# Batch 0 of a state-attention and Mish kernel: a finer hand-written order, word scaling for two slots at a time, and a state product in 256-column pieces

## The chip, the cores and the metric

The kernel runs on one core of a Trainium2 chip. The metric is the device time of one execution in microseconds (us). The median of three runs before the change is 707.46 us (705.67 to 708.41).

Five engines work side by side, each through its own queue in order: TensorE (PE: matrix products and transposes), VectorE (DVE), ScalarE (ACT: activations, copies, casts), GpSimd (POOL) and SyncE (SP), which here only issues DMAs. An engine waits at an instruction until what it needs is there, and all that stands behind it in its queue waits too.

## The reference

Two parts. First an attention between `x` (8 batches, 8 heads, 512 tokens, 64 wide) and a small `state` (32 rows per head), in both directions. Then a two-layer network over the joined result (8 x 544 rows, 512 wide, hidden 2048).

```python
scores  = scale * x @ state.T                 # per batch and head
a       = softmax(scores over the 32 state rows)
xread   = a @ state                           # 512 rows per head
scores2 = scale * state @ x.T
a2      = softmax(scores2 over the 512 tokens)
sread   = a2 @ x                              # 32 rows per head
rows    = concat([xread, sread], axis=2)      # -> (8 * 544, 512)

h   = rows @ w_in
out = (h * tanh(softplus(h))) @ w_out         # Mish, then the second product
```

Inputs are 64-bit floats; the result is 32-bit.

## The kernel before

**Weights.** `w_in` and `w_out` come as pairs of 32-bit words of 64-bit floats. The kernel makes 32-bit floats of them itself, in eight pieces each: `scale_high` (Prelu on the high word) and `round_low` (Copy with scale and bias on the low word) prepare the halves, and `join_words` on VectorE shifts and ors them together (`join_w_in`, `join_w_out`). For `w_out` a cast (`high_w_out`) and a subtraction (`low_w_out`) follow: products that need 32-bit accuracy are made of a high and a low part in the faster fp32r format, three matmuls for one.

**The state is folded into the weights.** The xread rows are never formed. `sw_slice(b, j)` multiplies batch `b`'s state, laid out as blocks by `state_blocks`, with piece `j` of `w_in` (the state product, tiles `swp`) and splits the result into `swh` (ACT) and `swl` (DVE). Eight small matmul positions of the array, 64 rows by 32 columns each, work side by side in it; one such fp32 matmul shows as two instructions. `gemm1(b, j)` then multiplies the transposed attention weights (`ah`, `al`) with it: twelve matmuls of 512 columns into two PSUM tiles `ph`. Mish on ACT makes `g` of them, DVE splits `g` into `gh` (cast) and `gl` (subtraction), and `gemm2` adds its product with piece `j` of `w_out` into four accumulators `acc`: 24 matmuls, six for each tile of 128 tokens. One `j` is called a slot; a batch has eight (`SLOTS`). The sread rows of all batches are collected in `srT` and go through the network at the end (`gemm1_s`).

**The attention of a batch** (`attention`): transposes of x, scores, the softmax over state rows (`soft1_...`), the softmax over tokens (`soft2_...`), its transposes (`e2_transposed`), the read-out (`sread`) and its transpose (`sreadT`). For batches 0 and 1, x is transposed on PE; from batch 2 on it is loaded in another layout (`xq`) and transposed on DVE.

**Buffers** that matter here: two PSUM tiles `m` serve all small products (transposes of x, scores, state product, read-out); two `ph`; one `g`; two each of `gh`, `gl`, `swh`, `swl`; one joined `w_out` piece (`wt`); five `t` for the attention's temporaries; two `raw` for pieces of `w_in` as loaded. A load into a `raw` buffer can be issued only when the piece in it has been joined, and all DMAs stand in SP's queue in the order in which they are written. Pieces 2 and 3 of `w_in` lie where `w_out` 6 and 5 come later, and `w_out` 7 comes where batch 0's x lies.

**The order.** The program is planned by a scheduler that orders instructions by its own estimate of time. For batch 0 that is overridden: while `InOrder.on` is true, each instruction of PE, DVE and ACT is made to follow the one traced before it on the same engine, so these three queues run in the order in which lines 586 to 665 call them. In slots 1 to 7 that is the same pattern each time: the words of one piece of `w_in` (`words`, two halves) and one of `w_out`, from slot 3 on the low half of `w_out` on GpSimd; the joins; two tiles of the slot before's second product; mish and `gh`; the next state product; the other two tiles; `low_w_out` and `gl`; the next first product. Pieces of batch 0's second softmax and of batch 1's attention are put in at slots 3 to 7. What belongs to batch 1 and later and is traced after `InOrder.on = False` is free: the planner may put it into the three queues wherever it finds room, also between the ordered instructions.

Prelu and Exp belong to one table of ACT, Mish to another, and changing costs an `ACT_TABLE_LOAD`; Copy and casts stand in either. `FILL` matmuls without use keep PE busy at the start.

From batch 1 on a slot leaves the second product `LAG` slots behind, and a state product covers two slots: 512 columns, 16 matmul instructions.

Of the kernel before, what the change touches and what calls it, by code (L numbers as in the profile page):

```python
# [30 lines left out]
def as_f32(ap):  # L31
    return ap.bitcast(F32)

# [27 lines left out]
def state_attention_mish_kernel(ctx, tc, x, state, w_in, w_out, out):  # L61
# [70 lines left out]
    def scale_words(raw, pool_rounds=False):  # L132
        if pool_rounds:
            round_low(raw, True)
        scale_high(raw)
        if not pool_rounds:
            round_low(raw)

# [81 lines left out]
    def attention(b, sn, xq=None):  # L220
# [4 lines left out]
        def x_transposed(c):  # L225
# [17 lines left out]
        def scores():  # L243

            pss = [misc(f"sc_{b}_{u}") for u in range(2)]
            for c in range(NC):
                o = slice(c * NS, (c + 1) * NS)
                for kc in range(2):
                    kp = slice(kc * 2 * P, (kc + 1) * 2 * P)
                    for u in range(2):  # L250
                        last["PE"] = pe.matmul(
                            pss[u][o, kp], bds[b][half(u), kc, o], xTs[c][half(u), kp],
                            start=True, stop=True)

# [3 lines left out]
            for u in range(2):  # L258
# [4 lines left out]
                else:  # L263
                    act.mul(o, i, 0.125)

# [14 lines left out]
        def soft2_e(kc):  # L280
            e2 = temp(f"e2_{b}_{kc}")
            sm = pool.tile([P, 1], F32, tag="sm", name=f"sm_{b}_{kc}")
            act.activation(e2, sc[kc], AF.Exp, bias=nms[kc], accum_out=sm)
            dve.tensor_scalar_add(sm, sm, 1e-9)
# [3 lines left out]

        def soft2(kc):
            soft2_m(kc)  # L290
            soft2_e(kc)

        def e2_transposed(kc):
            e2 = e2s[kc]
            pt = misc(f"e2p_{b}_{kc}")
            for t in range(NT):
                pe.transpose(pt[:, t * P:(t + 1) * P], e2[:, t * P:(t + 1) * P], ident)
            e2T[kc] = temp(f"e2T_{b}_{kc}", (P, NT, P))
            act.copy(e2T[kc].rearrange("p t n -> p (t n)"), pt)

        e1s = {}
# [4 lines left out]
        e1, small = [], {}  # L306
# [11 lines left out]
        def soft1_e():  # L318
            e1.extend(temp(f"e1_{b}_{kc}") for kc in two)
            for n in ("mx", "s1", "r1"):  # L320
                small[n] = [pool.tile([P, 16], F32, tag=n, name=f"{n}_{b}_{kc}") for kc in two]
            src = e1
            if b == 0:
                src = [misc(f"scT_{b}_{kc}") for kc in two]
            for kc in two:
                if b == 0:
                    transposed(src[kc], sc[kc])
                else:
                    dve.transpose(e1[kc], sc[kc])
            for kc in two:  # L330
                mx = small["mx"][kc]
                dve.tensor_reduce(mx, groups(src[kc]), AX.X, ALU.max)
                dve.tensor_sub(groups(e1[kc]), groups(src[kc]), wide(mx))
                act.activation(e1[kc], e1[kc], AF.Exp)

        def soft1_n():
            sm, r1 = small["s1"], small["r1"]

            def total(kc):
                dve.tensor_reduce(sm[kc], groups(e1[kc]), AX.X, ALU.add)  # L340

            def guard(kc):
                dve.tensor_scalar_add(sm[kc], sm[kc], 1e-9)

            def turn(kc):
                dve.reciprocal(r1[kc], sm[kc])

            def norm(kc):
                dve.tensor_mul(groups(e1[kc]), groups(e1[kc]), wide(r1[kc]))

            for step, kc in ((total, 0), (guard, 0), (total, 1), (turn, 0), (guard, 1), (norm, 0), (turn, 1), (norm, 1)):
                step(kc)

        def soft1_a():
            for kc in two:
                if b == 0:
                    at = ps_acc.tile([P, 512], F32, tag="acc", name=f"at_{b}_{kc}")
                    transposed(at, e1[kc])
                else:
                    at = temp(f"at_{b}_{kc}")  # L360
                    dve.transpose(at, e1[kc])
                hi = pool.tile([P, S], F32R, tag=f"ah{kc}", name=f"ah_{b}_{kc}")
                lo = pool.tile([P, S], F32R, tag=f"al{kc}", name=f"al_{b}_{kc}")
                act.copy(hi, at)
                dve.tensor_sub(lo, at, as_f32(hi))
                aT[kc] = (hi, lo)

        def soft1():
            soft1_e()
            soft1_n()  # L370
            soft1_a()

        def sread(kc):
            pr = misc(f"srp_{b}_{kc}")
            for t in range(NT):
                for h4 in range(4):
# [6 lines left out]
                    )  # L383
            if kc == 0:
# [3 lines left out]
        def sreadT():  # L388
            pt = misc(f"srTp_{b}")[:, :P]
            pe.transpose(pt, srd[0].rearrange("p k d -> p (k d)"), ident)  # L390
            ptv = pt.rearrange("p (c n) -> p c n", c=NC)
            hi, lo = (t[..., b * NS:(b + 1) * NS] for t in srT)
            act.copy(hi, ptv)
            dve.tensor_sub(lo, ptv, as_f32(hi))

        xt, s_, s1, s2, e2t, sr = x_transposed, scores, soft1, soft2, e2_transposed, sread
        own = dict(xt=xt, s=s_, s1e=soft1_e, s1n=soft1_n, s1a=soft1_a, m2=soft2_m, e2=soft2_e,
                   e2t=e2t, sr=sr, srT=sreadT, fill=fill, aT=aT)
        ahead = [
            lambda: (state_blocks(b, sn), xt(0), xt(1)),  # L400
            lambda: (xt(2), xt(3)),
            lambda: s_(),
            lambda: (s1(), s2(0), s2(1)),
        ]
        read = [
            lambda: (e2t(0), e2t(1)),
            lambda: sr(0),
            lambda: sr(1),
            lambda: sreadT(),
# [329 lines left out]
```

## Time and profile before

| | |
|---|---|
| Runs | 707.46 us median of 3 (705.67 to 708.41) |
| Profiled execution | 703.54 us, of which 701.8 lie between its first and last instruction (the span) |
| Granted TensorE clock | 0.997 |
| Busy, share of the span | PE 97%, weight loads 74%, DVE 49%, ACT 38%, POOL 1% |
| Batch 0 | first product at 20.5 us; batch 1's first product at 108.1 us |
| Loads | 32 MB read; 399 GB/s between 10 and 30 us, 30 to 46 between 70 and 100 |

A row of the timeline gives the start and length in us, the engine, the source line (here the recording helper's, so tiles tell more), the operation, the tiles out <- in with their shape, and how many were merged (x4). What stands in brackets is the engine's idle time just before and what ended it. Matmuls overlap: twelve of 0.39 us follow each other at 0.23. Groups and windows sum such rows.

### The profile page before, as it was taken

To read this page: it belongs to the slowest core of one execution; us is meant where nothing else is said; L and a number is where in the kernel's file an instruction comes from. 1 tells how busy PE (TensorE), PEld (TensorE's weight loads), DVE (VectorE), ACT (ScalarE), POOL (GpSimd) and SP (SyncE) were. 2 spreads that over 40 slices of the span, in tenths; PEclk is the share of its full clock that TensorE was granted. 3 is DMA by queue.
4 is the path that set the end of the run, shared out by engine and by line. 5 is a ranking of instruction groups with operands and counts; after the bars stand their busy time and mean duration, and the time that the engine had idled before them with its cause. 6 is when DMAs were issued, how large, how long until landed. Compare 5 with 4: busy or idle time off the path is not lost.

```text
span 701.8 us, 10128 instructions
## 1 busy us (share of the span) xinstructions
PE 681.9 (97%) x4194; PEld 516.0 (74%) x4194; DVE 346.9 (49%) x520; ACT 264.6 (38%) x417; POOL 8.0 (1%) x11
## 2 busy tenths in 40 slices
PE   8999877999999999999999999999999999999997
PEld 7777554777677777777777777777777788977785
DVE  4886578365438423753357333842374334332221
ACT  4987735235235312551146122631245123212110
POOL 0020000000000000000000000000000000000000
PEclk9999999999999999999999999999999999999999
DMA  9964210340213010311022011301010001001001
GB/s 329 389 246 131 37 25 2 88 97 0 66 66 49 7 61 20 83 23 61 5 82 41 19 42 65 49 8 61 10 52 0 1 1 61 1 5 26 1 0 61
DMA packets 74926, 41.56 MB, mean 59 GB/s; under 512 B 56192, under 2 KB 64384, under 8 KB 74880
## 3 DMA queue, kind: packets, MB, share of 16 engines
q1 hardware_dynamic: 74592, 40.85, 19.9%
q8 instruction: 33, 0.54, 0.3%
q14 instruction: 13, 0.11, 0.1%
q10 hardware_dynamic: 288, 0.07, 0.0%
HBM read 31.98 MB, written 8.91 MB: 58 GB/s over the span
## 4 chain that ended last, share of the span: by engine, by line
PE 94%; ACT 2%; DVE 2%; issue 0%; DMA 0%; POOL 0%; ACTq 0%; POOLq 0%; DVEq 0%
PE acc L53 51%; PE ph L53 25%; PE swp L53 5%; PE ph_s L53 3%; PE acc_s L53 3%; PE sc L53 1%; PE srp L53 1%; PE e2p L53 1%; DVE e L53 1%; PE st L53 1%; ACT L53 1%; ACT wir L53 1%; PE xTp L53 1%; PE warm L53 0%; DVE s L53 0%
## 5 line engine op out<-in xcount | busy, mean ns | idle before, releaser
L53 PE MATMUL acc<-wo,gh 128*128 128x512 f32 x1024 | 326.9, 400 | 0.0
L53 PEld LDWEIGHTS acc<-wo,gh 128*128 128x128 f32 x1024 | 188.2, 188 | 69.0 <-issue 23.0
L53 PE MATMUL acc<-wo,gl 128*128 128x512 f32 x512 | 201.7, 396 | 0.0
L53 ACT ACTIVATE g<-ph 128x512 f32<-128x512 f32 x128 | 74.2, 597 | 224.8 <-DVE gl L53 147.0
L53 DVE CAST gh<-g 128x1024 fp32r<-128x1024 f32 x64 | 44.2, 691 | 161.3 <-PE acc L53 142.6
L53 PEld LDWEIGHTS acc<-wo,gl 128*128 128x128 f32 x512 | 96.2, 188 | 23.4 <-DVE gl L53 0.8
L53 PE MATMUL ph<-ah,swh 128*128 128x512 f32 x256 | 84.8, 404 | 7.0 <-ACT swh L53 3.5
L53 DVE TENSOR_TENSOR gl<-g,gh 128x1024 fp32r<-128x1024 f32 x64 | 78.3, 1223 | 4.9
L53 PE MATMUL ph<-al,swh 128*128 128x512 f32 x256 | 79.9, 393 | 0.0
L53 PE MATMUL ph<-ah,swl 128*128 128x512 f32 x256 | 79.4, 392 | 0.0
L53 DVE TENSOR_TENSOR swl<-swp,swh 128x512 fp32r<-128x512 f32 (+1 forms) x72 | 42.5, 624 | 49.7 <-ACT swh L53 49.1
L53 PEld LDWEIGHTS ph<-ah,swh 128*128 128x128 f32 x256 | 47.7, 189 | 21.8 <-ACT swh L53 4.4
L53 ACT ACT_TABLE_LOAD x39 | 50.0, 1283 | 26.8 <-PE e2p L53 14.1
L53 PEld LDWEIGHTS ph<-al,swh 128*128 128x128 f32 x256 | 48.3, 189 | 11.2 <-DVE xT L53 0.8
L53 PEld LDWEIGHTS ph<-ah,swl 128*128 128x128 f32 x256 | 47.7, 188 | 10.7
L53 ACT CAST swh<-swp 128x512 fp32r<-128x512 f32 (+1 forms) x72 | 35.6, 547 | 24.5 <-PE swp L53 24.5
L53 PE MATMUL swp<-w_in_sb,bd 64*32 64x512 f32 (+1 forms) x576 | 39.9, 554 | 0.4 <-DVE w_in_sb L53 0.3
L53 DVE TENSOR_TENSOR wl<-w_in_sb,wh 128x512 fp32r<-128x512 f32 x16 | 11.1, 692 | 29.1 <-PE ph_s L53 25.2
L53 ACT COPY o<-acc 128x512 f32<-128x512 f32 x16 | 9.4, 586 | 41.5 <-PE acc L53 27.9
L53 DVE STREAM_TRANSPOSE xT<-xq 128x512 f32<-128x512 f32 x24 | 24.2, 1083 | 0.1
L53 DVE COPY o<-acc 128x512 f32<-128x512 f32 x16 | 11.0, 688 | 24.2 <-DMA out_dram<-o 15.9
L53 PE MATMUL acc_s<-wo,gh_s 128*128 128x512 f32 x64 | 20.3, 395 | 0.0
(77 smaller groups left out, 490.0 us busy)
## 6 DMA issues: line engine op xcount, KB each, us to landing
x<-in_x_dram SPq DMA_DIRECT2D x32, 256.0 KB, 3.8
wir<-in_moe_w_in_dram SPq DMA_DIRECT2D x16, 512.0 KB, 9.2
wor<-in_moe_w_out_dram SPq DMA_DIRECT2D x16, 512.0 KB, 6.4
out_dram<-o SPq DMA_DIRECT2D x32, 256.0 KB, 2.2
xq<-in_x_dram SPq DMA_DIRECT2D x192, 32.0 KB, 2.3
out_dram<-o_s SPq DMA_DIRECT2D x8, 64.0 KB, 1.7
sn<-in_state_dram SPq DMA_DIRECT2D x14, 32.0 KB, 4.7
sn<-in_state_dram ACTq DMA_DIRECT2D x2, 32.0 KB, 3.4
```

The source lines that it names most:

```text
L53: made = method(*args, **kwargs)
```

## The change

Batch 0's order is no longer a loop but a list of steps, each a name and a piece number. A step that has several parts on several engines is a generator: its first mention in the list runs it up to the first `yield`, the next mention runs the next part. So a transposition on PE and the copy of its result on ACT can stand at different places. The second product is cut into its four tiles (`by_tiles`). Capital letters are batch 1's attention.

- Words: `hi`/`ci` are the high and low half of a `w_in` piece, `ho`/`co` of a `w_out` piece. They are spread so that in slots 3, 5 and 7 mish follows without an exponential or a high half (both of the other table) since the mish before. All run on ACT; `round_low` on GpSimd is no longer called.
- Batch 1's softmax over state rows begins in slot 6 (`TR`, `EX`, `NO`), its end (`PR`) is in slot 7. The transposes of its x stand between tiles of second products.
- The second softmax of batch 0 begins in slot 0 (`mm0`), its exponentials are in slots 1 and 2, and its read-out in slot 3.
- `sw_slice` makes a product over two slots in two passes of 256 columns, where it was one of 512; its two casts come ahead of its two subtractions. Batches 1 to 7 use this too.

```diff
     def sw_slice(b, j, n=2):
-        f = slice(j * 2 * P, (j + n) * 2 * P)
         pw = [misc(f"swp_{b}_{j}_{kc}")[:, :n * 2 * P] for kc in range(2)]
-        for c in range(NC):
-            o = slice(c * NS, (c + 1) * NS)
-            for kc in range(2):
-                last["PE"] = pe.matmul(
-                    pw[kc][o, :], bds[b][half(kc), kc, o], w_in_sb[half(kc), c, f], start=True, stop=True)
+        for i in range(n):
+            f, to = (slice(q * 2 * P, (q + 1) * 2 * P) for q in (j + i, i))
+            for c in range(NC):
+                o = slice(c * NS, (c + 1) * NS)
+                for kc in range(2):
+                    last["PE"] = pe.matmul(
+                        pw[kc][o, to], bds[b][half(kc), kc, o], w_in_sb[half(kc), c, f], start=True, stop=True)
+        yield
...
         for kc in range(2):
             last["swh"] = act.copy(hi[:, kc], pw[kc])
+        yield
+        for kc in range(2):
             last["swl"] = dve.tensor_sub(lo[:, kc], pw[kc], as_f32(hi[:, kc]))
...
+    def mish_high(j):
+        g = mish(0, j, phs.pop(j))
+        yield
+        gs[j] = (g, *high_g(f"0_{j}", g))
+        pending.append((0, (2 * j, 2 * j + 1), gs[j][1:], NT))
+
+    def by_tiles(j):
+        for t in range(NT):
+            second((t,), t + 1 < NT)
+            yield
...
-    for j in range(1, SLOTS):
-        if j < 7:
-            words(j + 1, j, j > 2)
-        if j == 6:
-            words(None, 7, True)
-        if j + 1 < SLOTS:
-            join_i(j + 1)
...
-        second((0, 1), True)
-        low = finish()
-        if j + 1 < SLOTS:
-            sw.update(sw_slice(0, j + 1, 1))
-        else:
-            sw.update(sw_slice(1, 0))
-        second((2, 3))
...
+    steps = {
+        "hi": lambda i: scale_high(raws[i]), "ci": lambda i: round_low(raws[i]),
+        "ji": lambda i: join_w_in(i, raws.pop(i)),
+        "ho": lambda o: scale_high(rawo[o]), "co": lambda o: round_low(rawo[o]), "jo": join_o,
+        "lo": lambda o: low_w_out(o, wfull.pop(o)),
+        "sw": lambda j: sw_slice(0, j, 1), "p": first,
+        "m": mish_high, "lg": lambda j: low_g(*gs.pop(j)), "g": by_tiles,
+        "fill": lambda i: at0["fill"](FILL[i], accs[0][NT - 1]), "acc": lambda _: new_accs(0, NT),
+        "next": lambda _: sw_slice(1, 0),
+        **{n: f for n, f in at0.items() if n not in ("fill", "aT")},
+        **{n.upper(): f for n, f in at1.items() if n not in ("fill", "aT")},
+    }
+    begun = {}
+    for step in """
+            x0 x1 x0 x1 st st x2 x3 x2 x3 sc sc sc hi0 ci0 tr0 tr1 tr0 tr1 ex0 ex1 acc fill0 hi1 ci1 no
+            no ji0 pr0 pr1 pr0 pr1 pr0 pr1 fill1 sw0 fill2 sw0 sw0 p0
+            co0 mm0 ho0 ji1 m0 sw1 jo0 fill3 jo0 sw1 hi2 ci3 m0 sw1 ci2 lo0 lg0 co1 ji2 ho1 p1
+            m1 g0 g0 sw2 g0 sw2 g0 co2 jo1 jo1 ee0 m1 sw2 hi3 lo1 lg1 p2
+            mm1 ho2 g1 ji3 ee1 g1 sw3 hi4 sw3 m2 g1 ci4 g1 co3 jo2 sw3 jo2 m2 ee1 ee0 et0 lg2 lo2 ji4 p3
+            et0 sr0 et1 m3 sr0 ho3 g2 g2 sw4 g2 et1 hi5 sw4 ci5 hi6 jo3 co4 jo3 sr1 g2 sw4 m3 p4
+            ho4 lg3 ji5 lo3 ho5 sr1 sw5 jo4 g3 ST rt sw5 sw5 g3 jo4 m4 p5
+            rt ST rt X1 m4 lg4 X0 co5 X1 X0 g3 lo4 X2 g3 jo5 m5 ci6 ji6 X3 X2 sw6 g4 X3 SC sw6 ci7 sw6
+            ho6 jo5 SC g4 SC p6
+            lo5 ho7 g4 m5 lg5 TR0 TR0 g4 hi7 ji7 co6 TR1 TR1 sw7 jo6 EX0 g5 EX1 sw7 g5 jo6 sw7 m6 g5 lo6
+            m6 next NO g5 lg6 p7
+            NO m7 PR0 PR0 g6 g6 PR0 PR1 co7 jo7 m7 next jo7 lo7 g6 next PR1 g6 PR1 lg7
+            """.split():
+        what, i = re.fullmatch(r"([a-zA-Z]+)(\d*)", step).groups()
+        if step not in begun:
+            begun[step] = steps[what](int(i or 0))
+        if hasattr(begun[step], "send"):
+            next(begun[step], None)
```

The attention's functions (`x_transposed`, `scores`, `soft1_...`, `soft2_e`, `e2_transposed`, `sread`, `sreadT`), `state_blocks` and `join_o` get a `yield` between their parts on different engines; `soft1_e` becomes `soft1_t` (transpose, maximum, subtraction) and `soft1_x` (exponential), for each half on its own. What each computes is unchanged. `fill` stays at the same numbers.

More of the change, by code (lines that the diff above doesn't have):

```diff
@@ L1 @@
+import re
 from contextlib import ExitStack, contextmanager
@@ L32, in as_f32, with whole @@
     return ap.bitcast(F32)
+def whole(*pieces):
+    for piece in pieces:
+        for _ in piece:
+            pass
 def half(par):
@@ L336, in soft1_n @@
[L336 to L371, printed above, removed]
+        def soft1_t(kc):
+            e1[kc] = temp(f"e1_{b}_{kc}")
+            small[kc] = [pool.tile([P, 16], F32, tag=n, name=f"{n}_{b}_{kc}") for n in ("mx", "s1", "r1")]
+            if b == 0:
+                src = misc(f"scT_{b}_{kc}")
+                transposed(src, sc[kc])
+            else:
+                src = e1[kc]
+                dve.transpose(src, sc[kc])
+            yield
+            mx = small[kc][0]
+            dve.tensor_reduce(mx, groups(src), AX.X, ALU.max)
+            dve.tensor_sub(groups(e1[kc]), groups(src), wide(mx))
@@ new lines, in soft1_x, with soft1_n, total, guard @@
+        def soft1_x(kc):
+            act.activation(e1[kc], e1[kc], AF.Exp)
+        def soft1_n():
+            sums, turned = ([small[kc][i] for kc in two] for i in (1, 2))
+            def total(kc):
+                dve.tensor_reduce(sums[kc], groups(e1[kc]), AX.X, ALU.add)
+            def guard(kc):
+                dve.tensor_scalar_add(sums[kc], sums[kc], 1e-9)
+            def turn(kc):
+                dve.reciprocal(turned[kc], sums[kc])
+            def norm(kc):
+                dve.tensor_mul(groups(e1[kc]), groups(e1[kc]), wide(turned[kc]))
+            for step, kc in ((total, 0), (guard, 0), (total, 1), (turn, 0), (guard, 1), (norm, 0)):
+                step(kc)
+            yield
+            turn(1)
+            norm(1)
@@ new lines, in soft1_a @@
+        def soft1_a(kc):
+            if b == 0:
+                at = ps_acc.tile([P, 512], F32, tag="acc", name=f"at_{b}_{kc}")
+                transposed(at, e1[kc])
+            else:
+                at = temp(f"at_{b}_{kc}")
+                dve.transpose(at, e1[kc])
+            yield
+            hi = pool.tile([P, S], F32R, tag=f"ah{kc}", name=f"ah_{b}_{kc}")
+            lo = pool.tile([P, S], F32R, tag=f"al{kc}", name=f"al_{b}_{kc}")
+            act.copy(hi, at)
+            yield
+            dve.tensor_sub(lo, at, as_f32(hi))
+            aT[kc] = (hi, lo)
@@ L373, in sread, with soft1 @@
+        def soft1():
+            whole(*(soft1_t(kc) for kc in two))
+            for kc in two:
+                soft1_x(kc)
+            whole(soft1_n(), *(soft1_a(kc) for kc in two))
         def sread(kc):
@@ L383, in sread @@
                     )
+            yield
             if kc == 0:
@@ L426, in sw_slice @@
             last["swh"] = act.copy(hi[:, kc], pw[kc])
+        yield
+        for kc in range(2):
             last["swl"] = dve.tensor_sub(lo[:, kc], pw[kc], as_f32(hi[:, kc]))
-        return {j + i: [t[:, :, i * 2 * P:(i + 1) * 2 * P] for t in (hi, lo)] for i in range(n)}
+        for i in range(n):
+            sw[j + i] = [t[:, :, i * 2 * P:(i + 1) * 2 * P] for t in (hi, lo)]
     def take_g(g, k, ph):
@@ new lines, in first @@
+    def first(j):
+        phs[j] = gemm1(0, j, aTs[0], sw)
+    def mish_high(j):
+        g = mish(0, j, phs.pop(j))
+        yield
+        gs[j] = (g, *high_g(f"0_{j}", g))
[3 more added lines that the diff above has]
+            second((t,), t + 1 < NT)
+            yield
+    sw, aTs, phs, gs = {}, {}, {}, {}
+    InOrder.on = True
+    (at0, _, _), (at1, ahead1, read) = attention(0, sn0), attention(1, sn1)
+    aTs[0], aTs[1] = at0["aT"], at1["aT"]
@@ L665, in state_attention_mish_kernel, with soft2_1 @@
+    def soft2_1():
+        for kc in range(2):
+            at1["mm"](kc)
+            whole(at1["ee"](kc))
     InOrder.on = False
@@ L671, in state_attention_mish_kernel @@
         slots += [(b, j) for j in range(SLOTS)]
-    todo = [lambda: [at1[p](kc) for p in ("m2", "e2") for kc in range(2)]] + read
+    todo = [soft2_1] + read
     xqs = {2: new_xq(2)}
```

147 lines of the change are left out of this document (24 added, 123 removed).

## The prediction

> **What bounds the kernel now.** I read the page first, then busy time by stretch, then TensorE's idle places in the timeline, and last what ended them.
>
> ```profile
> span 701.8 us, 10128 instructions
> PE 681.9 (97%) x4194; PEld 516.0 (74%) x4194; DVE 346.9 (49%) x520; ACT 264.6 (38%) x417; POOL 8.0 (1%) x11
> 20.51:108.13 87.62, 76.74 (x535) 55.84 (x534) 64.52 (x89) 62.86 (x86) 7.28 (x5) 1.00 0.47 152
> 112.00:600.00 488.00, 488.00 (x3026) 367.05 (x3025) 240.81 (x373) 168.62 (x280) 0.00 (x0) 1.00 0.16 40
> ```
>
> In the last two rows come the stretch, its length, and the busy time of PE, PEld, DVE, ACT and POOL. PE works through 112 to 600 us without a gap. Batch 0's ordered part, from its first product at 20.51 to batch 1's first at 108.13, has 76.74 busy of 87.62: 10.88 idle. What a new order of batch 0 can win lies there and just behind it. These are PE's idle places from 20 to 112 us (in brackets the idle time and what ended it):
>
> ```profile
> 66.52 0.66 PE L53 MATMUL xTp<-ident,x 128*128 128x128 f32 x4 [0.68 <-ACT xT L53]
> 73.33 0.66 PE L53 MATMUL xTp<-ident,x 128*128 128x128 f32 x4 [2.85 <-DVE srT_l L53]
> 87.42 0.67 PE L53 MATMUL swp<-w_in_sb,bd 64*32 64x256 f32 x16 [0.31 <-DVE w_in_sb L53]
> 94.63 0.78 PE L53 MATMUL ph<-ah,swh 128*128 128x512 f32 x2 [3.55 <-ACT swh L53]
> 108.13 0.73 PE L53 MATMUL ph<-ah,swh 128*128 128x512 f32 x2 [3.50 <-ACT ah L53]
> 110.26 1.97 PE L53 MATMUL e2p<-ident,e 128*128 128x128 f32 x8 [1.40 <-ACT e L53]
> ```
>
> The first five make 0.68 + 2.85 + 0.31 + 3.55 + 3.50 = 10.89, the whole idle time of the stretch. Behind 108.13 come three more losses: the 1.40; the eight transposes of that row, which wait in their middle for the second exponential (1.97 against 1.03 for the eight at 56.19: 0.94); and a state product that ran as two halves, each nearly as long as a whole one (1.06 + 1.06 against 1.09: 1.03).
>
> ```profile
> 56.19 1.03 PE L53 MATMUL e2p<-ident,e 128*128 128x128 f32 x8
> 113.66 1.06 PE L53 MATMUL swp<-w_in_sb,bd 64*32 64x512 f32 x8
> 116.25 1.06 PE L53 MATMUL swp<-w_in_sb,bd 64*32 64x512 f32 x8
> 139.48 1.09 PE L53 MATMUL swp<-w_in_sb,bd 64*32 64x512 f32 x16
> ```
>
> That is 1.40 + 0.94 + 1.03 = 3.37, so 14.26 us are there to be won in all; the rest of PE's work stays.
>
> **How the new order is costed.** Each step of the list issues on known engines, and each engine runs its steps in the list's order. So I laid both orders out on three lines: an instruction starts when its engine is free and, 0.03 us after their end, its inputs and buffers are there. The durations are those of the timeline of before, of ACT, of DVE, and of PE's chain of waits:
>
> ```profile
> 24.14 1.08 ACT L53 ACTIVATE g<-ph 128x512 f32<-128x512 f32 x2
> 25.11 0.66 ACT L53 CAST swh<-swp 128x256 fp32r<-128x256 f32 x2
> 25.78 1.28 ACT L53 ACT_TABLE_LOAD   x1
> 27.08 2.18 ACT L53 ACTIVATE wir<-wir 128x1024 f32<-128x1024 f32 x2
> ```
>
> ```profile
> 22.86 1.23 DVE L53 SCALAR_TENSOR_TENSOR w<-wor 128x1024 uint32<-128x1024 uint32 x1 [0.47 <-ACT wor L53]
> 24.12 0.70 DVE L53 CAST wo<-w 128x1024 fp32r<-128x1024 f32 x1
> 25.86 0.75 DVE L53 TENSOR_TENSOR swl<-swp,swh 128x256 fp32r<-128x256 f32 x2
> 26.53 1.22 DVE L53 TENSOR_TENSOR wo<-w,wo 128x1024 fp32r<-128x1024 f32 x1
> 87.28 1.30 DVE L53 STREAM_TRANSPOSE e<-scs 128x512 f32<-128x512 f32 x2
> 89.18 0.69 DVE L53 TENSOR_TENSOR e<-e,mx 128x512 f32<-128x512 f32 x1
> ```
>
> ```profile
> 139.55 1.02 PE swp L53 x16
> 140.57 5.79 PE acc L53 x24
> 146.59 1.06 PE sc L53 x32
> 155.96 2.73 PE ph L53 x12
> ```
>
> Two instructions of one engine overlap by about 0.1 us, so a word half costs ACT 1.06 and a 1024-wide subtraction DVE 1.13. As a check, the old order so laid out starts slot 7's product at 93.42 and batch 1's at 106.66; the trace has 94.63 and 108.13. The layout is short by 1.2 and 1.5 us, so I take from it the stalls of the new order and not its clock times, and set them against PE's busy 76.74, which the change leaves as it is.
>
> **Words by table, and no GpSimd.** Between the same two products ACT loaded its table this often:
>
> ```profile
> L53 ACT ACT_TABLE_LOAD x14 | 18.0, 1283 | 0.3
> 32.09 1.43 POOL L128 TENSOR_SCALAR wor<-wor 128x1024 uint32<-128x1024 uint32 x1 [30.78 <-DMA wor<-in_moe_w_out_dram]
> 32.58 1.49 DVE L53 CAST wo<-w 128x1024 fp32r<-128x1024 f32 x1
> ```
>
> The last of the 14 began at the stretch's very end, so 13 count. In the new list the mish of two slots stands in one table's turn three times (2 and 3, 4 and 5, 6 and 7), and I count nine loads: 4 x 1.28 = 5.1 us less. Five word halves come over from POOL: 5 x 1.06 = 5.3 more. ACT's 62.86 stays. DVE gains: the cast of 0.70 at 24.12 took 1.49 at 32.58, while POOL ran. Neither engine has more than 65 us of work against PE's 77, so as sums they hide all of it; only the places where a step comes late count.
>
> **The order, stall by stall.** The old 2.85 was a chain through one pair of PSUM buffers: PE's transposes of x waited for the read-out subtraction, which DVE had queued behind a join that waited for ACT's words. The list puts these transposes between tiles of the second product, and words earlier, so this goes; so do the 0.68 and the 0.31. The 3.55 was slot 7's product behind a table load, two exponentials, a load, mish and two casts; now both exponentials and slot 7's casts end at 84.1 in the layout, and PE reaches that product at 89.6: 5.5 us of cover. The 3.50 was batch 1's softmax, normalized in slot 7 behind the second product's work; normalizing now begins among slot 6's last steps.
>
> What is late next, in the layout: (1) slot 1's words are five halves behind one table load (27.08 + 3 x 1.06 + 0.08 = 30.34 for w_in 2, join 1.23 to 31.60); PE is there at 31.21 and waits 0.42. (2) The first read-out product waits 0.36 for the copy of the transposed exponentials behind two words. (3) Slot 6's state product waits 0.73 for the last x copy's buffer. With hand-overs of 0.05 to 0.1 that is 2.0 us up to batch 1's first product, which so starts at 20.51 + 76.74 + 2.0 = 99.25 and not 108.13. (4) From slot 6 on DVE is nearly full: from the first transpose of batch 1's scores to the subtraction for the second half (al) it has 19.8 us of work and 2.2 of waits, and al comes out 1.70 behind the fourth matmul of batch 1's first product, which needs it; the rest of that product stands behind.
>
> **The free part.** From batch 1 on, order is the planner's, and it puts free work into the ordered queues:
>
> ```profile
> 82.69 1.28 DVE L53 TENSOR_REDUCE nm<-scs 128x1 f32<-128x512 f32 x2 [1.81 <-ACT scs L53]
> 113.20 2.98 DVE L53 STREAM_TRANSPOSE xT<-xq 128x512 f32<-128x512 f32 x3
> ```
>
> The two maxima went into slot 6 and three transposes of batch 2 into the end of slot 7. The new order can't be known for this. Bounds: nothing, where it fits into waits, to the maxima and four such transposes in front of al, 1.3 + 4 x 1.0 = 5.3. I take the maxima alone, 1.2, since they are ready just then and the transposes stood behind al before. So 1.7 + 1.2 = 2.9 stays behind the start of batch 1, for 3.37 of before.
>
> **State product in 256 columns.** Each of the products of 16 matmuls becomes 32 of half the width.
>
> ```profile
> L53 PE MATMUL swp<-w_in_sb,bd 64*32 64x512 f32 x448 | 34.6, 601 | 0.0
> 59.95 0.66 PE L53 MATMUL swp<-w_in_sb,bd 64*32 64x256 f32 x16
> 60.54 0.72 PE L53 MATMUL acc<-wo,gh 128*128 128x512 f32 x2
> ```
>
> 448 / 16 = 28 products. The nearest row is the scores: 32 matmuls of this very size, 1.06 against 1.02, so 0.04 x 28 = 1.1. The upper bound is two separate products of 60.54 - 59.95 = 0.59: 0.16 x 28 = 4.5; the lower is nothing, since the same columns stream. I take 1.1.
>
> The Trainium skill (TensorEngine Tiling (Array Packing), Instruction Overhead) speaks against this part: each matmul carries some 60 cycles, so a short dimension should not be cut. At the 2.4 GHz of its page Trainium Kernel Development and Optimization (NeuronCore Architecture) that is 25 ns, and 448 more of them, if paid one by one, 11.2 us by this estimate: the sum would be +1.9. The 1.06 of the scores does not bear that out; eight tiles run side by side there.
>
> **Sum.** -10.89 + 2.0 - 3.37 + 2.9 + 1.1 = -8.3. The profiled execution took 703.54 (span 701.8 and 1.7 around it) and would take 695.3. The median of the runs shown is 707.46, 3.9 above it; against that, the forecast is 699.2.
>
> **Rivals.** (A) Better cover: the planner sets transposes or tiles into the 1.7, nothing is inserted, and the product costs nothing: -10.89 + 2.0 - 3.37 = -12.3, 695.2. For it: PE has independent work by then; against: DVE is as full.
>
> (B) A load decides. The list scales w_in 6 in slot 3 and no longer in slot 5; its load can only be issued when join 4 has freed the buffer, at 48.9 + 1.2 in the layout, and ACT wants it at 54.7.
>
> ```profile
> wir<-in_moe_w_in_dram SPq DMA_DIRECT2D x4, 512.0 KB, 3.7
> wir<-in_moe_w_in_dram SPq DMA_DIRECT2D x16, 512.0 KB, 9.2
> ```
>
> The four loads of 45 to 60 us landed after 3.7 us; at the median of all, 9.2 (some 10 for the second half), ACT waits, with slot 4's words, casts and mish behind it, and the layout starts batch 1 4.1 later: 703.3. Against it: SP's queue and the DMA engines are quiet by then.
>
> (C) The change doesn't do what it says, as the planner spends it: the 5.3 of free work goes ahead of al, so 7.0 stays behind the start for 2.9: 703.3 too.
>
> (D) Slower: matmuls of the 256-column product pay one by one, as the skill's rule has it. Priced by rows, the second half of the columns costs a full 0.59 and the first gets no shorter: 0.59 x 28 = 16.5, so 707.46 - 9.4 + 16.5 = 714.6. It turns the sign when a product takes 0.33 more (9.4 / 28), 1.35 in place of 1.02. Against it stands the scores' 1.06.
>
> **How the numbers follow.** Forecast 0.54, A 0.20, B 0.10, C 0.10, D 0.06. The forecast's own range is 696 to 703. The range reaches to A and past B and C with the runs' spread of 1.4 on either side, 693.5 to 705.5; D is left out. A measurement of this kernel tells about 0.5% from no change, so faster is below 703.9: the forecast and A nearly whole, and over half of B and C, 0.83; the rest of these and a part of D make 0.11 within 0.5%, and D 0.06 slower.
>
> **What would show it.** Right: batch 1's first product near 99; PE without an idle place of over 1 us before it; nine table loads in that stretch; the 4th matmul of that product waiting for al; no POOL row behind the identity's; the 32 matmuls of a product in 1.0 to 1.1. Wrong: an idle place of 3 us or more in slots 3 and 4 ended by the words of w_in 6 (B); transposes of batch 2 among DVE's last steps of slot 7 (C); products of over 1.3 us (D); or PE idle anywhere in 130 to 600 us, which I don't expect at all.

## The result and the profile after

| | before | after |
|---|---|---|
| Runs | 707.46 us median (705.67 to 708.41) | 684.59 us median (684.14 to 684.81) |
| Profiled execution | 703.54 us, span 701.8 | 684.41 us, span 682.6 |
| Ratio | | 0.968, 95% interval 0.9666 to 0.9697 |

The change makes the kernel faster by 22.9 us. The forecast was 699.2 us, a gain of 8.3, with a range that ended at 693.5: the sign was right and the size far too small. The two headline lines of the page of after:

```profile
span 682.6 us, 11019 instructions
PE 673.9 (99%) x4642; PEld 522.7 (77%) x4642; DVE 342.5 (50%) x520; ACT 263.5 (39%) x418; POOL 0.7 (0%) x6
```

PE's share went from 97 to 99%, but its busy time also fell, 681.9 to 673.9, though no product was taken out. That is the first sign that more than idle places changed. Busy time by stretch shows where: first the three stretches of after, then the two of before that the prediction did not show. The columns are the stretch, its length, the busy time of PE, PEld, DVE, ACT and POOL, the granted clock, the DMA share and GB/s.

```profile
19.57:96.46 76.89, 76.30 (x552) 56.44 (x550) 62.81 (x90) 64.19 (x88) 0.00 (x0) 1.00 0.55 179
96.46:179.63 83.17, 82.98 (x620) 62.35 (x619) 46.06 (x75) 30.21 (x53) 0.00 (x0) 1.00 0.21 53
179.63:682.00 502.37, 498.31 (x3326) 390.41 (x3324) 222.98 (x336) 159.08 (x266) 0.00 (x0) 1.00 0.13 34
```

```profile
108.13:194.47 86.34, 84.94 (x551) 61.64 (x552) 48.91 (x77) 32.37 (x54) 0.00 (x0) 0.98 0.20 51
194.47:701.00 506.53, 502.72 (x2962) 384.01 (x2960) 222.88 (x336) 159.27 (x266) 0.00 (x0) 1.00 0.13 33
```

The borders are batch 0's first product, batch 1's first product and batch 2's first mish. Set against the prediction's terms (the last stretch is taken to the end of the span):

| Stretch | predicted | measured | difference |
|---|---|---|---|
| up to batch 0's first product | 0 | 19.57 - 20.51 = -0.94 | -0.9 |
| to batch 1's first product | -10.89 + 2.0 = -8.9 | 76.89 - 87.62 = -10.73 | -1.8 |
| to batch 2's first mish | -3.37 + 2.9 + 0.2 = -0.3 | 83.17 - 86.34 = -3.17 | -2.9 |
| from there to the end | +0.9 (256 columns) | 502.97 - 507.33 = -4.36 | -5.3 |
| span | -8.3 | -19.2 | -10.9 |

The first row is chance: runs of the same new order start batch 0's first product at 19.5 to 20.5, those of the old order at 19.4 to 20.5. In the second row 1.4 of the 1.8 are waits that did not come (0.59 of the 2.0), and 0.44 is faster work (PE busy 76.30 for 76.74). The other 3.7 us of the 14.6 by which the forecast missed the median do not stand in these two traces at all: the profiled execution of before is 3.9 us faster than its median, that of after 0.2.

PE's idle places in after, from the timeline of PE between 19.5 and 130 us (the two rows with a bracket are the only ones), with the rows around batch 1's first product:

```profile
30.71 0.67 PE L61 MATMUL swp<-w_in_sb,bd 64*32 64x256 f32 x16 [0.16 <-DVE w_in_sb L61]
...
70.16 0.91 PE L61 MATMUL swp<-w_in_sb,bd 64*32 64x256 f32 x16 [0.43 <-DVE w_in_sb L61]
...
96.46 0.63 PE L61 MATMUL ph<-ah,swh 128*128 128x512 f32 x2
96.92 1.08 PE L61 MATMUL acc<-wo,gh 128*128 128x512 f32 x4
...
99.14 1.10 PE L61 MATMUL acc<-wo,gh 128*128 128x512 f32 x4
100.08 1.03 PE L61 MATMUL e2p<-ident,e 128*128 128x128 f32 x8
```

Of 10.88 us of idle time 0.59 are left. Batch 1's first product is still interrupted, since its `al` is late, but now PE does eight matmuls of the second product of slot 7 in between (1.08 + 1.10 us) and the eight transposes run in 1.03 us without a wait, where they took 1.97 behind a wait of 1.40. The rows of ACT and DVE that answer to the prediction's steps, from the timeline of after:

```profile
54.36 1.17 ACT L61 ACTIVATE wir<-wir 128x1024 f32<-128x1024 f32 x1 [0.89 <-DMA wir<-in_moe_w_in_dram]
76.99 1.24 DVE L61 TENSOR_REDUCE nm<-scs 128x1 f32<-128x512 f32 x2
94.73 1.28 ACT L61 ACT_TABLE_LOAD   x1
99.98 0.68 DVE L61 TENSOR_TENSOR al<-at,ah 128x512 fp32r<-128x512 f32 x1
```

And two groups of that first stretch and of the whole span (count, busy time, mean ns):

```profile
L61 ACT ACT_TABLE_LOAD x10 | 12.8, 1283 | 0.2
masks.py:199 POOL TENSOR_SCALAR_AFFINE_SELECT ident<-ident 128x128 f32<-128x128 f32 x1 | 0.3, 292 | 0.1
```

### The profile page after: what moved, and what is told of

Read it like the earlier page. It is cut to its first block, busy times and chain, and to the rows that moved or that the text cites. A ratio compares the mean times of both kernels' runs of the same rounds, so it can differ in the third digit from the quotient of the medians.

```text
span 682.6 us, 11019 instructions
## 1 busy us (share of the span) xinstructions
PE 673.9 (99%) x4642; PEld 522.7 (77%) x4642; DVE 342.5 (50%) x520; ACT 263.5 (39%) x418; POOL 0.7 (0%) x6
## 3 DMA queue, kind: packets, MB, share of 16 engines
q1 hardware_dynamic: 74592, 40.85, 20.5%
## 4 chain that ended last, share of the span: by engine, by line
PE 89%; DMA 4%; ACT 3%; DVE 2%; SPq 1%; issue 1%; DVEq 0%; ACTq 0%
PE acc L61 49%; PE ph L61 24%; PE swp L61 5%; PE ph_s L61 3%; PE acc_s L61 3%; DMA wir<-in_moe_w_in_dram 2%; PE srp L61 1%; DMA wor<-in_moe_w_out_dram 1%; PE e2p L61 1%; PE sc L61 1%; PE st L61 1%; ACT wir L61 1%; ACT L61 1%; DVE w_in_sb L61 1%; DVE e L61 1%
## 5 line engine op out<-in xcount | busy, mean ns | idle before, releaser
L61 PE MATMUL swp<-w_in_sb,bd 64*32 64x256 f32 x1024 | 39.9, 383 | 0.7 <-DVE w_in_sb L61 0.6
L61 PEld LDWEIGHTS swp<-w_in_sb,bd 64*32 64x32 f32 x1024 | 16.0, 105 | 18.8 <-issue 11.4
```

The source lines that it names most:

```text
L61: made = method(*args, **kwargs)
```

## The experiments

Gain and loss are told against the kernel before, which ran beside them (706.7 to 707.1 us median in each group), or against the new order, 684.7. "Distance" is the mean distance between the starts of two consecutive 512-wide matmuls of the first or second product, worked out from some 1,390 such pairs of each trace between 150 and 550 us. "Lost at low clock" is, over the stretches of 2 us from 20 to 160 us, PE's busy time by one less the granted clock.

**First question: the product in 256 columns, alone and taken away.** Four kernels: each order with each form of `sw_slice`. The edit is the loop of the diff above, put into the old order or taken out of the new one; the other two kernels are before and after as they are.

> The kernel before, unchanged, profiled again beside the three others. Matmuls of the two large products follow each other at a mean of 231.7 ns in the first profile of before and at 229.4 ns in the one of after, at every stage. Theory 1 (the pitch belongs to the chip or the execution, not to the kernel): its profile here shows the same pitch as the three others of this call, whatever it is; batch 1's first product at 107 to 108 us. Theory 2 (the pitch belongs to the kernel's 512-column product): 231 to 232 here and in the other kernel with 512 columns, 229 to 230 in the two with 256.

> The kernel before with nothing but the state product of batches 1 to 7 in two passes of 256 columns. Theory 1: a product takes 1.02 us as before, batch 1 starts at 107 to 108 us as before, and the time is within 1 us of the old order with 512. Theory 2: 5 to 8 us faster than the old order with 512, spread evenly over batches 1 to 7.

> The kernel after with the state product back in one pass of 512 columns. Theory 1: batch 1 starts at 96 to 97 us, and the time is within 1 us of the new order with 256 columns. Theory 2: 5 to 8 us slower than that, with batch 1 still at 96 to 97 us.

> The kernel after, unchanged, beside the other three. Both theories: batch 1 starts at 96 to 97 us. Theory 1: against the old order with 512 columns the gain is 14 to 16 us, all of it before 200 us. Theory 2: 19 to 23 us, of which 5 to 8 come after 200 us.

| | median, us | ratio to before | distance, ns |
|---|---|---|---|
| old order, 512 | 707.0 | 1.000 (0.9988 to 1.002) | 231.6 |
| old order, 256 | 705.8 | 1.000 (0.9982 to 1.0016) | 231.4 |
| new order, 512 | 684.7 | 0.970 (0.9672 to 0.9721) | 229.2 |
| new order, 256 | 684.8 | 0.970 (0.9672 to 0.9729) | 229.4 |

The product costs nothing and brings nothing, in either order. One product of 16 matmuls in the old order and one of 32, from the chains of waits of old_order_512 and old_order_256:

```profile
102.32 1.13 PE swp L53 x16
```

```profile
102.42 1.13 PE swp L53 x32
```

The prediction's +1.1 and rival D fall with this. And another riddle shows: the matmuls of the long products follow each other 2.2 ns sooner on average in the new order, in all batches, also in batches 3 to 6, whose program differs in `sw_slice` alone. One second product of 24 matmuls in the steady part, from the chains of waits of before and of after:

```profile
295.53 5.79 PE acc L53 x24
298.39 5.72 PE acc L61 x24
```

It is neither the chip (all four ran on one) nor the 256 columns, so both theories that were written down for the distance fall.

**Second question: where the 2.2 ns come from, and GpSimd.** In the built kernels the buffers `g`, `w`, `gh` and `gl` lie 64 bytes higher in the new order. `nm`, the two maxima (2 x 32 bytes), is first written in slot 0 there and so gets its place ahead of these four; in the old order it got a place behind them. `gh` and `gl`, the weights of the second product, thus begin at 0 modulo 512 bytes in the old order and at 64 in the new. The pieces of `w_out` stay at 128, `swh`, `swl`, `ah` and `al` at 0.

```diff
 # old_order_shifted: ahead of slot 0, nm gets its place early
     finish = product(0, 0)
+    dve.memset(pool.tile([P, 1], F32, tag="nm", name="nm_first"), 0.0)
 # new_order_unshifted: nm fills 2 x 256 bytes
-            nm = nms[kc] = pool.tile([P, 1], F32, tag="nm", name=f"nm_{b}_{kc}")
+            nm = nms[kc] = pool.tile([P, 64], F32, tag="nm", name=f"nm_{b}_{kc}")[:, :1]
 # old_order_nopool: the low halves of w_out 3 to 7 on ACT
-            words(j + 1, j, j > 2)
+            words(j + 1, j)
-            words(None, 7, True)
+            words(None, 7)
 # new_order_pool: the same halves on GpSimd
-"co": lambda o: round_low(rawo[o]),
+"co": lambda o: round_low(rawo[o], o > 2),
```

> The kernel before; the only edit makes the first one-column tile nm (written once with zero by VectorE) in slot 0, so that its two 32-byte buffers come to lie ahead of w, g, gh and gl in SBUF and not behind them: these four move up by 64 bytes, as they did in the kernel after. Theory 3 (the 1% slower matmuls of the old order come from where gh and gl lie): the mean distance of matmuls falls from 231.6 to about 229.4 ns in all batches, 5 to 6 us are gained, and batch 1 starts where it did, at 107 to 109 us. Theory 4 (it comes from the order, say from what the other engines do meanwhile): 231.6 as before, time within 1 us of before.

> The kernel after; the only edit pads nm to 256 bytes a buffer, so that g, w, gh and gl lie 512 bytes further up than in the kernel before, on a multiple of 512 as there, and not 64 bytes off it. Theory 3: 231.6 ns instead of 229.4, 5 to 6 us slower than the kernel after, 690 us. Theory 4: 229.4 ns and 684 to 685 us.

> The kernel before; the low halves of w_out pieces 3 to 7 run on ScalarE, all else as it is. In the old order ScalarE's mish stands behind the words of its slot, so each of slots 3 to 6 starts up to 1.06 us later where ScalarE is the late one: 0 to 4 us slower. VectorE's slow casts go away, which gives back up to 1 us. If GpSimd itself were the cause of the gain, this would be several us faster.

> The kernel after; the low halves of w_out pieces 3 to 7 go back to GpSimd, all else as it is. If giving up GpSimd is worth anything by itself, some casts and joins on VectorE take 0.2 to 0.9 us longer where GpSimd runs beside them, and the time is 1 to 3 us above that of the kernel after. If the order hides it, within 1 us: ScalarE has five halves of 1.06 us less to do.

| | median, us | ratio to before | distance, ns |
|---|---|---|---|
| old_order_shifted | 702.1 (698.1 to 703.4) | 0.993 (0.9902 to 0.9957) | 229.3 |
| new_order_unshifted | 688.9 (688.7 to 689.5) | 0.9746 (0.9731 to 0.976) | 231.4 |
| old_order_nopool | 706.5 (706.1 to 710.0) | 1.000 (0.9987 to 1.0016) | 231.6 |
| new_order_pool | 685.4 | 0.969 (0.9677 to 0.9706) | 229.4 |

Placement works both ways: it gives the old order 5.0 us (707.1 to 702.1; 3 to 7 by the interval of the ratio) and takes 4.2 from the new one (684.7 to 688.9). One batch apart, the same mish in the steady part (timelines of ACT), first before and old_order_shifted, then after and new_order_unshifted:

```profile
265.33 0.60 ACT L53 ACTIVATE g<-ph 128x512 f32<-128x512 f32 x1 [1.30 <-DVE gl L53]
...
341.50 0.60 ACT L53 ACTIVATE g<-ph 128x512 f32<-128x512 f32 x1 [1.30 <-DVE gl L53]
```

```profile
266.77 0.60 ACT L53 ACTIVATE g<-ph 128x512 f32<-128x512 f32 x1 [1.29 <-DVE gl L53]
...
342.28 0.60 ACT L53 ACTIVATE g<-ph 128x512 f32<-128x512 f32 x1 [1.29 <-DVE gl L53]
```

```profile
249.78 0.60 ACT L61 ACTIVATE g<-ph 128x512 f32<-128x512 f32 x1 [1.30 <-DVE gl L61]
...
325.37 0.60 ACT L61 ACTIVATE g<-ph 128x512 f32<-128x512 f32 x1 [1.30 <-DVE gl L61]
```

```profile
250.93 0.60 ACT L61 ACTIVATE g<-ph 128x512 f32<-128x512 f32 x1 [1.30 <-DVE gl L61]
...
327.08 0.60 ACT L61 ACTIVATE g<-ph 128x512 f32<-128x512 f32 x1 [1.30 <-DVE gl L61]
```

The batch takes 76.17, 75.51, 75.59 and 76.15 us: it goes with the placement, not with the order. Giving up GpSimd's five halves is worth 0.7 us at most in the new order (684.4 to 685.5 with them) and nothing that shows in the old one. What is left for the order itself, at equal placement, is 707.1 - 688.9 = 18.2 us, twice the forecast, so a second cause was missing.

**Third question: the clock behind an idle place.** Granted clock (the third number from the right) by stretch, in before and in old_order_512, the same program on another run:

```profile
108.00:110.00 2.00, 0.73 (x2) 0.30 (x2) 1.31 (x2) 1.97 (x3) 0.00 (x0) 0.98 0.00 0
110.00:112.00 2.00, 1.74 (x9) 1.74 (x9) 1.18 (x5) 1.96 (x6) 0.00 (x0) 0.50 0.00 0
112.00:114.00 2.00, 2.00 (x10) 1.17 (x12) 2.00 (x3) 0.64 (x2) 0.00 (x0) 0.66 0.00 0
```

```profile
96.00:98.00 2.00, 2.00 (x6) 1.62 (x5) 2.00 (x2) 0.00 (x0) 0.00 (x0) 0.50 0.11 16
98.00:100.00 2.00, 2.00 (x7) 1.59 (x7) 0.22 (x1) 1.03 (x2) 0.00 (x0) 0.68 0.00 0
...
110.00:112.00 2.00, 1.09 (x3) 0.37 (x3) 1.19 (x3) 1.99 (x4) 0.00 (x0) 0.50 0.00 0
112.00:114.00 2.00, 2.00 (x9) 2.00 (x10) 1.42 (x6) 1.74 (x5) 0.00 (x0) 0.50 0.00 0
114.00:116.00 2.00, 2.00 (x8) 0.92 (x11) 2.00 (x3) 0.55 (x1) 0.00 (x0) 0.50 0.00 0
```

Behind its waits of 3.5 us PE ran at half clock, behind one of them in the one run, behind both in the other. The Trainium skill (TensorE: Matmul & The Clock Gate, What's actually happening) has this rule: a window of about 3.4 us without work halves the clock, and the window runs freely, so that its place against the program differs from run to run. The second half is what the two runs show. Between 20 and 160 us no run of the new order but the one below shows a stretch under 0.97. Two kernels test what it costs:

```diff
 # old_order_filled: useless matmuls ahead of the products of slot 7 and of batch 1,
 # into free columns of the state product's tile, and into a tile of their own
+        if j == 6:
+            keep(spare[0], 24)
+        if j == 7:
+            keep(misc("keep")[:, :P], 24)
         if j + 1 < SLOTS:
             finish = product(0, j + 1)
 # new_order_late_softmax: normalization of batch 1 at the end of slot 7
-            m6 next NO g5 lg6 p7
-            NO m7 PR0 PR0 g6 g6 PR0 PR1 co7 jo7 m7 next jo7 lo7 g6 next PR1 g6 PR1 lg7
+            m6 next g5 lg6 p7
+            m7 g6 g6 co7 jo7 m7 next jo7 lo7 g6 next g6 NO NO PR0 PR0 PR0 PR1 PR1 PR1 lg7
```

> The old order, with 24 matmuls of the identity with itself (128 columns, no use) set in front of slot 7's first product and 24 in front of batch 1's first product, into free columns of PSUM. They do not shorten either wait (3.55 and 3.50 us before): batch 1's first product stays at 108 to 110 us. Theory 1 (what the old kernel loses at its idle places is the wait and, behind it, TensorE at a granted clock of 0.50): the clock stays at 1.00 from 90 to 120 us, the eight transposes behind the first product take 1.0 to 1.4 and not 1.97, and the time falls by the half-clock stretches, 1.5 to 4.3 us: 703 to 705, with a spread under 1 us. Theory 2 (the half clock costs nothing, since PE waits for DVE and ACT there anyway): 706.5 to 707.5, and the spread stays.

> The new order with batch 1's normalization and its transposes (NO, PR) put back to the end of slot 7, behind the second product, where the old order had them; all else is as in the new order. Theory 1 (that place in the list removes the 3.50 us idle place, and a wait of that length brings half clock with it): an idle place of 3 to 4.5 us comes back in front of batch 1's first product, ended by ScalarE's ah, the granted clock falls to 0.50 for some us behind it, and the time is 4.5 to 8 us above the new order's 684.7: 689 to 693. Theory 2 (the wait only costs itself): 687.7 to 689.2. Theory 3 (the finer list would hide it elsewhere, the move of the softmax does nothing): 684.5 to 685.5.

old_order_filled took 712.0 us (ratio 1.0068, 1.0043 to 1.0094), and does not answer the question: the fillers made waits of their own. From PE's timeline:

```profile
72.56 1.12 PE L53 MATMUL xTp<-ident,x 128*128 128x128 f32 x4 [2.32 <-DVE srT_l L53]
...
96.26 7.25 PE L53 MATMUL swp<-ident 128*128 128x128 f32 x48 [4.35 <-DVE swl L53]
...
112.92 5.52 PE L53 MATMUL keep<-ident 128*128 128x128 f32 x48
```

They waited for the subtraction that still read their tile, and 24 of them were 48 instructions and 5.5 us, longer than the wait that they should fill. The first row is of use all the same: a wait of 2.32 us, and the four transposes behind it took 1.12 for 0.66 (granted clock 0.65 from 72 to 74 us).

new_order_late_softmax took 692.4 us (692.35 to 692.75), 7.7 above the new order; theory 1 had said 4.5 to 8. Its idle places in PE's timeline, and the clock behind them:

```profile
102.55 1.22 PE L61 MATMUL ph<-ah,swh 128*128 128x512 f32 x2 [3.71 <-ACT ah L61]
104.68 1.97 PE L61 MATMUL e2p<-ident,e 128*128 128x128 f32 x8 [0.91 <-ACT e L61]
```

```profile
102.00:104.00 2.00, 1.22 (x2) 0.50 (x2) 1.31 (x2) 1.97 (x3) 0.00 (x0) 0.50 0.00 0
104.00:106.00 2.00, 1.32 (x6) 1.32 (x7) 0.76 (x5) 1.96 (x6) 0.00 (x0) 0.50 0.00 0
106.00:108.00 2.00, 2.00 (x8) 1.44 (x6) 2.00 (x3) 1.06 (x2) 0.00 (x0) 0.50 0.04 8
```

The old place of the softmax brings the old picture back: 3.71 + 0.91 us of waits, 2.5 lost at half clock, and the 1.97 of the transposes, which ran in 1.03 in after. So this one move in the list is worth about 7.7 of the new order's 18. The half clock by itself is told apart by the next group.

**Fourth question: the half clock by itself, and what of the placement counts.**

```diff
 # old_order_kept_busy: fillers that wait for nothing; zeros added to an accumulator
+    def keep(n):
+        for _ in range(n):
+            pe.matmul(accs[0][NT - 1][:, :P], zeros, ident, start=False, stop=False)
 # j == 5, ahead of batch 1's third transpose of x: keep(11); ahead of slot 7's and batch 1's products: keep(14)
 # new_order_gh_alone: nm fills 512 bytes (g and w at 0), w 128 more (gh and gl at 128)
+            nm = nms[kc] = pool.tile([P, 64], F32, tag="nm", name=f"nm_{b}_{kc}")[:, :1]
+        w = pool.tile([P, 2 * DM + 32], F32, tag="wt", name=f"w_{j}", bufs=1)
 # new_order_all_moved: nm fills 128 bytes, and ahead of everything
+    nc.gpsimd.memset(const.tile([P, 32], F32, name="spacer"), 0.0)
 # new_order_shift_128, _192, _256: nm fills 128, 192, 256 bytes ([P, 16], [P, 24], [P, 32])
```

> The old order with useless matmuls (zeros times identity, added to an accumulator, about 0.22 us each) in front of the three waits of 2.85, 3.55 and 3.50 us: 11, 14 and 14 of them, 2.4, 3.1 and 3.1 us, so that each ends before the wait does. Theory 1 (behind each of these waits TensorE runs at half clock for some us, in some runs behind one, in others behind all three, and that time is lost in full): batch 1's first product stays at 107 to 110 us, no stretch of 2 us from 20 to 160 us shows a clock under 0.97, and the time falls to 701 to 703, since the span of every old run less its loss at low clock was 699.4 to 700.2; the spread of the runs is under 1 us. Theory 2 (the lost clock is mostly hidden behind waits for DVE and ACT): 705.5 to 707.

> The new order with the maxima's buffer padded so that g, w, gh and gl lie another 64 bytes higher: gh and gl begin at 128 modulo 512 bytes, as the w_out pieces do (new order 64, old order 0). Theory 1 (the distance of two 512-wide matmuls, 231.6 ns at offset 0 and 229.3 at 64, depends on the offset of the weights to the moving rows, and is least where they agree): 226 to 228 ns and 679 to 682 us. Theory 2 (offset 0 is the one bad place, all others are as 64): 229.3 ns, 684.7. Theory 3 (the offset to swh, ah and w_in counts, all at 0): any value between 228 and 232, 681 to 690.

> The new order with g, w, gh and gl at 192 modulo 512 bytes (w_out pieces at 128, swh and ah at 0). Theory 1 (distance from the moving rows' offset counts, the same on either side, with a period of 256): as 64, 229.3 ns and 684.7 us. Theory 2 (another shape): anything from 228 to 231.5 ns, 681 to 689 us.

> As the last one with 256 modulo 512. Theory 1 (least distance where weights and moving rows agree): further from agreement than 128, so 229 to 231 ns and 684 to 688. Theory 2 (offset 0 is the one bad place): 229.3 ns, 684.7. Theory 3 (a period of 256 or less): as offset 0, 231.5 ns, 688.9.

> The new order with gh and gl at 128 modulo 512 bytes, but g and w (the buffers in front of them) at 0. Theory 1 (what counts is where TensorE's weights gh and gl lie): 228.6 ns between 512-wide matmuls and 683.0 us, as with all four at 128. Theory 2 (what counts is where g and w lie, which VectorE and ScalarE read and write meanwhile): 231.5 ns and 688.9 us, as with all four at 0.

> The kernel with gh and gl at 128 once more, and 128 bytes of spacer in front of everything, so that gh, gl and the w_out pieces all lie at 256 modulo 512 and swh, swl, ah at 128: all relations are kept, all absolute places moved. Theory 1 (the offset of the weights to the moving rows counts): 228.6 ns, 683.0 us. Theory 2 (the absolute place of gh and gl counts, 256 being as bad as 0): 231.5 ns, 689.0 us.

old_order_kept_busy took 703.6 us (702.6 to 704.7; twelve runs), before beside it 706.7 (703.1 to 709.7); ratio 0.9954, 0.9935 to 0.9972. Its timeline of PE:

```profile
91.07 3.29 PE L53 MATMUL acc<-ident,zeros 128*128 128x128 f32 x28
94.78 0.78 PE L53 MATMUL ph<-ah,swh 128*128 128x512 f32 x2 [0.42 <-ACT swh L53]
...
104.59 3.29 PE L53 MATMUL acc<-ident,zeros 128*128 128x128 f32 x28
108.27 0.74 PE L53 MATMUL ph<-ah,swh 128*128 128x512 f32 x2 [0.39 <-ACT ah L53]
110.40 1.36 PE L53 MATMUL e2p<-ident,e 128*128 128x128 f32 x8 [1.39 <-ACT e L53]
...
116.88 1.20 PE L53 MATMUL acc<-wo,gh 128*128 128x512 f32 x4 [0.48 <-DVE wo L53]
```

And the granted clock (the third number from the right) behind that product, where before had 0.50 and 0.66:

```profile
110.00:112.00 2.00, 1.55 (x10) 1.18 (x11) 1.04 (x5) 2.00 (x7) 0.00 (x0) 1.00 0.00 0
112.00:114.00 2.00, 2.00 (x13) 0.74 (x12) 2.00 (x3) 0.64 (x3) 0.00 (x0) 1.00 0.00 0
```

Batch 1's first product starts where it did (108.27), no useful work is taken away, and a kernel that computes 39 useless matmuls more is 3.1 us faster, since its clock stays at 1.00. The theory of a full loss had asked for 701 to 703, the one of a hidden loss for 705.5 to 707; the truth lies between. The traces show what each lost:

| | idle, 20 to 160 us | lost at low clock | span |
|---|---|---|---|
| before | 12.3 | 1.6 | 701.8 |
| old_order_256 | 13.1 | 3.3 | 703.4 |
| old_order_512 | 11.9 | 4.4 | 703.9 |
| old_order_nopool | 12.3 | 7.4 | 706.7 |
| old_order_kept_busy | 4.5 | 0 | 701.8 |
| after | 0.7 | 0 | 682.6 |

Span less loss is 699.4 to 700.2 in the first four, but 701.8 in the fifth: at full clock PE came to `wo` too early and waited 0.48 at 116.88, and the planner put a part of the read-out in front of the second product's rest. Some 1.6 to 2.4 us of the loss are thus hidden or given back, and how they divide stays open.

The placements, all with the new order:

| begin of gh, gl / w_out / g, w / swh, ah (modulo 512) | median, us | distance, ns |
|---|---|---|
| 0 / 128 / 0 / 0 (new_order_unshifted) | 688.9 | 231.4 |
| 64 / 128 / 64 / 0 (the change) | 684.7 | 229.3 |
| 128 / 128 / 128 / 0 (new_order_shift_128) | 683.0 (682.6 to 683.3) | 228.7 |
| 192 / 128 / 192 / 0 (new_order_shift_192) | 689.3 | 231.8 |
| 256 / 128 / 256 / 0 (new_order_shift_256) | 689.0 | 231.5 |
| 128 / 128 / 0 / 0 (new_order_gh_alone) | 683.1 | 228.7 |
| 256 / 256 / 256 / 128 (new_order_all_moved) | 682.9 | 228.7 |

Where `g` and `w` lie does not matter; what counts is `gh` and `gl`, and not by their own place (256 is bad in one row and good in the last) but against the rest. (The small buffers and `o` behind them move with every pad too; in old_order_shifted these stayed, with the same 229.3 ns.) Of the five offsets tried the best is the one at which `gh` and `gl`, the weights of the second product, begin as the `w_out` pieces do, its moving rows; but by less than theory 1 had asked (228.7 for 226 to 228 ns). 192 as bad as 256 is not symmetric about 128, so the theory of mere distance falls. 256 measures as 0 does, as a period of 256 or less would have it.

The mean hides a split. From one matmul of the second product to the next it is 232.8 ns before, 229.6 after, 229.1 in new_order_shift_128 and 233.3 in new_order_shift_192. From one of the first product to the next it is 229.5, 228.3, 227.5 and 229.0. The larger part is thus in the product that reads `gh` and `gl`. But the operands of the first product, `swh`, `swl`, `ah` and `al`, lie at the same places in all rows but the last, and its pace moves too. So the offset of weights to their own moving rows can't be all of it; no run moves `w_out` alone, and the cause behind the offset stays open. (`w_in` begins at 128, not at 0 as one expectation has it.)

new_order_shift_128 is a version that beats both kernels: 683.0 us, ratio to before 0.9661 (0.9644 to 0.9677), 1.6 us below the change.

## Why the prediction was wrong, point by point

**What held.** The five idle places before batch 1's first product and the losses just behind it were there to be won: 10.3 of the 10.9 us went, and only two short waits came in their place. The layout's new waits were real in kind but smaller: the 0.42 of slot 1 became 0.16, and slot 6's product waited 0.43, for its piece of `w_in` to be joined and not for a buffer; the 0.36 did not come. Table loads: nine before the one at 94.73, which stands for the fourteenth of before. ACT's sum, which was to stay, rose by 1.3 (62.86 to 64.19); no wait of PE ended with ACT. POOL shows nothing behind the identity. w_in 6's load was late (0.89 us of ACT, rival B in small), without a wait of PE.

**Step that failed first: "the rest of PE's work stays", with "PE's busy 76.74, which the change leaves as it is".** It does not: 512-wide matmuls follow each other at 229.3 ns and not at 231.6, from batch 0 to the end, since one small tile was created earlier and moved the weights by 64 bytes. Worth 4.2 us here. Behind 130 us the prediction looked only for idle PE, as a sign against it; the change there came as faster work. Nothing in the trace of before could show it; the order in which the change first writes its tiles could have shown that buffers move, though not what that is worth.

**Second: the sum set against the median by adding 3.9.** The 3.9 was taken for an offset that stays. Most of it was a loss of the old kernel alone: at half clock, which the profiled execution had by chance little of (1.6 us; other runs up to 7.4). Keeping the clock up takes 3.1 us from the old kernel's median. The spread was the sign: 705.67 to 708.41 before, 684.14 to 684.81 after. A wait of 3.5 us was priced at 3.5 us.

**Third: the +2.9 behind batch 1's start, and the 3.37 beside it.** `al` was late, and by more than laid out: it is ready at 100.66, and the fourth matmul of the product that starts at 96.46 would have been due near 97.15, so 3.5 us for 1.7 + 1.2 = 2.9. The maxima did go into DVE's chain in front of it (76.99), as the prediction took it. What failed is "the rest of that product stands behind" as a loss: the planner set eight ready matmuls of slot 7 into that wait, the transposes and the product's other half filled what was left, and PE is not idle there. So the cover of rival A held though its condition, nothing inserted, did not, and the term measured nothing. Of the 3.37, the 1.40 went; of the 1.03 about half is left, since the state product is still split (0.56 and 1.00 us in PE's chain, for 1.02 in one piece). The 0.94 of the old transposes was for about two thirds half clock: at full clock, behind the same wait, they took 1.36 and not 1.97.

**Fourth: +1.1 for the 256 columns.** It measured nothing, and neither did rival D's 16.5: 1.13 us for the product in either form. The rule of the Trainium skill that the prediction weighed against the change there (TensorEngine Tiling (Array Packing), Instruction Overhead) shows no cost in these runs; the sum by it would have been +1.8, not +1.9.

**In sum**, of the 22.9 us between the medians some 10.3 are waits before batch 1's first product, 4.2 placement, 3.1 half clock. Of the 5.3 that are left, batch 1's first stretch holds 3.17 at most (a part of it is already counted as clock and placement); two us or more the runs do not assign.

## What to carry to other kernels

Price a long wait of TensorE (2.3 to 3.7 us in these runs) with a chance of half clock behind it, and read a spread of the runs that the profile doesn't explain as a hint to look there: the granted clock by 2 us stretches shows it. When a change creates a tile earlier or with another size, buffers behind it can move, and the steady state can change with them; compare the distance of like matmuls in two traces before you credit the edit, and try a pad. Work that the planner may place freely can cover a late operand that a hand-made layout counts as a wait, as it did here.

## What the hardware showed that was not expected

- TensorE's pace depends on where its operands lie in SBUF: 228.7 to 231.8 ns for a 512-wide matmul over shifts of 64 bytes, 1% of the whole kernel. The Trainium skill (TensorE: Matmul & The Clock Gate, Step-by-step: what each phase is for) says that weights and moving rows come through two read ports of their own and that loading weights takes nothing from the running matmul; the runs show that the place of `gh` and `gl` (new_order_gh_alone) changes the pace, also that of the first product, which does not read them. The mechanism was not found.
- Waits of 3.5 us were followed by the half clock in some runs and not in others at the same place. A wait of 2.32 us was enough once (old_order_filled), while one of 2.33 at the same place in old_order_512 was not; behind waits of 3.08 and 3.31 (old_order_256, old_order_nopool) the clock was 0.55 and 0.54 from 74 to 76 us. These last waits are below the 3.4 us of the Trainium skill's rule (TensorE: Matmul & The Clock Gate, What's actually happening), so a window of that length without any work does not account for them.
- Useless matmuls in its waits made the old kernel faster: 706.7 to 703.6 us.
